# Three opening groups of idle TensorE products: six of 512 columns each become twelve of 256 columns

## The chip, the cores and the metric

The kernel runs on one core of a Trainium2 chip. The metric is the device time of one execution in microseconds (us); before the change it is 158.09 us, the median of three runs that lie between 158.01 and 158.14 us. One more execution was taken under the hardware profiler. The core has four engines that compute and one that only moves data: TensorE (PE; its weight loads are listed apart as PEld), VectorE (DVE), ScalarE (ACT), GpSimd (POOL) and SyncE (SP). An entry such as PEldq or DVEq is the sequencer of that engine, the part that reads the engine's instruction list and hands the instructions out.

## The reference

Two layers follow each other. The first is a sorted block attention: for each of 4 batches and 8 heads an 8 by 8 matrix is normalized five times over rows and columns, mixes the eight blocks of 96 tokens of K and V, and each block of Q attends to its mixed block. The second is a gated layer whose gate is a product over the sequence.

```python
for _ in range(5):
    P = np.exp(P - np.max(P, axis=-1, keepdims=True))
    P = P / (np.sum(P, axis=-1, keepdims=True) + 1e-09)
    P = P / (np.sum(P, axis=-2, keepdims=True) + 1e-09)
k_sorted = np.einsum('bhij,bhjcd->bhicd', P, k_b)      # v_sorted alike
scores = scale * np.matmul(q_b, k_sb.transpose(0, 1, 2, 4, 3))
attn = softmax(scores);  x = np.matmul(attn, v_sb)     # x: 4 x 768 x 512
h = np.maximum(x @ w_in, 0.0);  u, v = h[..., :512], h[..., 512:]
v_n = (v - mean(v)) / np.sqrt(var(v) + 1e-06)
v_s = np.einsum('ts,bsd->btd', w_spatial, v_n) + b_spatial[None, :, None]
out = (u * v_s) @ w_out                                # 4 x 768 x 512
```

## The kernel before, in words

The program is one long unrolled list of units. ORDER (from line 17) names them in the order in which they are issued, `run` (L785) takes them one by one, and each engine receives its own instructions in that order; nothing is reordered later. Loads and stores go through the queues of POOL, SP and, at the end, ACT. A unit's arguments begin with the PSUM tile (ps0 to ps3) or the engine that empties it.

**The opening.** `CO` fills the tile `warm` with zeros. `SK` is the normalization, a chain between ACT and DVE. `L` issues the loads of q, k, v and of the weights from POOL's queue. `DM:ps:n:w` (`u_DM`, L223) issues n idle products of w columns, each with its own load of the same 128 columns of `warm` as weights; they write to a PSUM tile whose content nobody reads. Three such groups, on ps0, ps2 and ps1, stand first in TensorE's list. Behind them come `QT` (L314, transposes of Q), two more groups on ps0 and ps3, `QT` twice, `PR` (L256, the mixing matrices), a sixth group, and `KT` and `VT` (L383, mixed K and V). From there on TensorE has work without idle products: scores (`SC`, L442), their products with V (`AT`, L488), `XT` (L518), `VP` (L554), `UP` (L597), `SP` (L609) and `OP` (L636), interleaved over the four batches.

**The end.** The last batch is split finely. `SH` (L666) is the product over the sequence, eight groups of six products, in this order of PSUM tiles: 1, 2, 0, 2, 3, 1, 2, 3. The first four groups have 512 columns, the last four 256. DVE empties each into `z` (L672), and `GH` multiplies z by u into `gt` (L679) on POOL or DVE. A group that takes a PSUM tile for the second time waits until DVE has emptied it: the fourth group waits for the z of the second, the seventh for the z of the fourth, the eighth for the z of the fifth. `OH` (L686) is the output product, `OI` copies it out of PSUM and `OJ` (L698) stores it.

**The jump.** Between `SH`/`GH` and `OH` stands `IF`. A flag that was computed on the device says whether the inputs allow the short way of normalizing; each engine loads it (`LF`, L731) and then jumps at L794. If the flag is clear, the engines go to the block "usual", which holds the tail from `OH` on. If not, they run `general_path`, a second, safer version of the whole kernel. In the instruction list of each engine the general path stands directly behind the jump, and "usual" behind the general path, so that the usual case jumps over all of it. For TensorE, VectorE and ScalarE the unit `BH` (L734) gives the jump a hint that it will likely be taken.

A product of TensorE is two instructions, a weight load and the product. TensorE's compiled list has 1633 such pairs before the jump; a few semaphore and register instructions lie between them, seven of them between 20 us and the jump.

The lines that matter:

```python
223:    def u_DM(ps, n, w):
225:        for _ in range(int(n)):
226:            nc.tensor.matmul(t[:, 0, 0:int(w)], lhsT=warm[:, 0:128], rhs=warm[:, 0:int(w)], start=True, stop=True)
791:        head, tail = ORDER.split("IF")
794:        with tc.If(st["beyond"] < 1, preferred_fallthrough_block=False, label="usual") as usual:
```

Of the kernel before, what the change touches and what calls it, by code (L numbers as in the profile page):

```python
# [16 lines left out]

ORDER = """
IV:0 CO S0 SK:0 SK:1 LH:S:0 L:q:0:4:8 L:k:0:0:8 L:v:0:0:8 SK:2 IV:2 ID MA L:v:1:0:8 MC QC:A:1 SK:3 L:k:1:0:8 MB QC:A:0
DM:0:6:512 L:q:1:0:8 DM:2:6:512 DM:1:6:512 QT:3:A:0:1 SK:4 QT:2:A:0:3 DM:0:6:512 DM:3:6:512 L:wv QT:1:A:0:0 QT:2:A:0:2  # L20
PR:0 P0:0:2 L:wu P0:6:8 P0:2:4 DM:3:6:512 P0:4:6 PC:D KT:1:D:0:1 PD:1:4:8 KT:3:A:0:0 L:wsb L:wsa KT:0:D:0:3 KT:2:A:0:2
IV:1 L:v:2:0:8 VT:1:A:0:0 VT:3:D:0:1 PD:1:0:4 SC:0:0:0:0 SC:2:0:0:1 VB:1:D:0:0 L:k:2:0:8 VB:3:D:0:1 SC:0:0:1:0
VT:1:A:0:2 AT:2:0:0:0 VT:3:A:0:3 PD:2:4:8 AT:0:0:1:0 L:q:2:0:8 VM:1:A:1:0 VB:2:D:0:2 SC:3:0:1:1 XT:0:D:0:0:0
AT:1:0:0:1 SC:2:0:2:0 VM:3:A:1:3 VB:0:D:0:3 PD:2:0:4 SC:1:0:2:1 AT:2:0:2:0 KT:3:D:1:1 KT:0:D:1:2 SC:1:0:3:0 VM:2:A:1:1
SC:3:0:3:1 AT:1:0:1:1 KT:2:A:1:3 KT:0:A:1:0 AT:3:0:3:0 VM:1:A:1:2 PD:3:4:8 QQ:2:D:1:0 XT:3:D:0:1:0 L:k:3:0:8
AT:0:0:3:1 XT:1:A:0:0:2 QQ:2:A:1:2 AT:3:0:2:1 VP:1:A:0:0:1 XT:0:D:0:1:2 ST:0:1 VP:2:D:0:2 ST:0:0 SC:0:1:1:1 SC:3:1:2:1
L:q:3:0:8 VC:1:4:8 VP:1:D:0:4:5 SC:2:1:3:1 ST:0:4 ST:0:5 SC:3:1:3:0 VP:0:A:0:3 SC:2:1:0:1 ST:0:2 UP:1:A:0:1:1
AT:0:1:1:1 L:v:3:0:8 SC:3:1:0:0 ST:0:3 UP:2:A:0:0:0 AT:0:1:3:1 AT:1:1:2:1 LN:0:0:6 UP:3:A:0:0:1 AT:0:1:0:1 LA:0:5
WW:2:A:0 WW:1:D:4 XT:3:A:1:1:2 UP:0:A:0:1:0 LA:0:2 VC:1:0:4 AT:2:1:0:0 VM:1:A:2:1 BI WW:3:D:2 SC:0:1:2:0 VM:2:A:2:2
XT:1:D:1:1:0 LA:0:0 BH LA:0:4 LA:0:1 LA:0:3 VM:3:A:2:0 SC:0:1:1:0 VP:1:A:1:4:5 AT:2:1:3:0 AT:0:1:1:0 ST:1:5 SP:3:0:2  # L30
AT:0:1:2:0 L:wo SP:1:0:0 VM:2:D:2:3 SP:0:0:1 VC:2:4:8 XT:3:D:1:0:2 XT:1:A:1:0:0 VC:2:0:4 QQ:2:D:2:0 KT:0:A:2:1
KT:3:D:2:0 GT:D:0:0 QQ:1:D:2:2 KT:2:A:2:2 KT:0:A:2:3 PD:3:0:4 GT:P:0:2 VP:3:A:1:0:1 SC:1:2:0:1 SC:2:2:0:0 SP:0:0:3
ST:1:4 SC:3:2:2:1 SC:1:2:1:1 ST:1:1 VP:2:A:1:2:3 KT:3:D:3:2 QQ:0:D:3:0 ST:1:2 SC:1:2:3:0 UP:2:A:1:1:0 AT:0:2:0:1
GT:P:0:3 KT:3:A:3:0 ST:1:3 QQ:1:D:3:2 SC:0:2:3:1 AT:2:2:2:1 UP:3:D:1:0:1 VM:1:A:3:3 UP:0:A:1:0:0 AT:2:2:3:1
UP:3:A:1:1:1 GT:P:0:1 ST:1:0 LN:1:0:6 AT:2:2:1:1 AT:0:2:3:0 XD:2:1 LA:1:4 OP:1:0:0 AT:2:2:0:0 OE:A:0:0 OP:0:0:2
SC:2:2:2:0 LA:1:2 LA:1:5 OE:D:0:2 SC:1:2:1:0 LA:1:1 LA:1:0 LA:1:3 OP:3:0:4 AT:1:2:1:0 AT:0:2:2:0 SP:2:1:2 VM:0:D:3:1
VM:1:D:3:0 OE:A:0:4 VP:3:D:2:4:5 KT:0:A:3:1 KT:2:D:3:3 SP:1:1:3 VM:0:A:3:2 GT:D:1:3 OS:0:0 ST:2:4 SP:3:1:1 SC:2:3:3:1
SC:1:3:1:1 XD:2:0 OS:0:2 GT:D:1:2 ST:2:5 SP:0:1:0 VC:3:4:8 SC:3:3:2:1 SC:2:3:0:1 UP:1:D:2:1:0 GT:D:1:1 VC:3:0:4
VP:3:A:2:2:3 AT:1:3:3:1 GT:P:1:0 VP:2:A:2:0:1 ST:2:3 AT:1:3:2:1 AT:3:3:1:1 UP:0:A:2:1:1 OP:1:1:0 ST:2:0 ST:2:1 ST:2:2
OE:A:1:0 AT:2:3:0:1 LN:2:0:6 LA:2:1 UP:0:D:2:0:0 SC:1:3:0:0 LA:2:3 SC:3:3:1:0 LA:2:2 LA:2:5 LA:2:0 OP:2:1:4 AT:1:3:0:0  # L40
AT:3:3:1:0 XD:3:1 OE:A:1:4 OP:0:1:2 LA:2:4 SC:1:3:3:0 OE:D:1:2 SC:3:3:2:0 SP:2:2:2 AT:1:3:2:0 UP:0:A:2:0:1 AT:3:3:3:0
CK VP:2:A:3:4:5 GT:D:2:2 OS:1:2 SP:1:2:1 ST:3:5 OS:1:4 XD:3:0 SP:3:2:3 SP:2:2:0 ST:3:4 CF:3 GT:D:2:1 GT:P:2:3
UP:0:A:3:1:0 VP:2:D:3:2:3 VP:3:A:3:0:1 ST:3:0 ST:3:1 ST:3:2 UP:2:A:3:0:1 GT:P:2:0 LF OP:1:2:2 ST:3:3 OE:A:2:2 LN:3:0:6
OP:0:2:0 LA:3:4 LA:3:5 OS:2:2 OE:A:2:0 UP:3:D:3:1:1 LA:3:2 LA:3:0 OP:2:2:4 LA:3:3 OE:A:2:4 LA:3:1 OS:2:4 UP:0:A:3:0:0
SH:1:3:3:0 GH:P:3:3:0 SH:2:3:0:0 GH:D:3:0:0 SH:0:3:1:0 SH:2:3:2:0 SH:3:3:1:1 GH:P:3:1:0 SH:1:3:0:1 GH:P:3:2:0 OS:1:0
GH:P:3:1:1 SH:2:3:3:1 SH:3:3:2:1 OS:2:0 GH:P:3:0:1 GH:D:3:2:1 GH:D:3:3:1 OS:0:4 IF OH:1:3:2:0:512:0:4
OH:2:3:3:0:512:0:4 OH:0:3:4:0:256:0:4 OI:A:3:2:0:512 OI:A:3:3:0:512 OH:3:3:5:0:256:0:4 OI:D:3:4:0:256 OI:D:3:5:0:256
OJ:3:2:0:512:S OJ:3:3:0:512:S OJ:3:4:0:256:S OJ:3:5:0:256:A OH:2:3:5:256:512:0:4 OH:1:3:1:0:512:0:4
OH:3:3:4:256:512:0:4 OI:D:3:5:256:512 OI:A:3:1:0:512 OJ:3:5:256:512:S OI:A:3:4:256:512 OJ:3:4:256:512:S OJ:3:1:0:512:A
OH:2:3:0:0:512:0:4 OI:A:3:0:0:512 OJ:3:0:0:512:S  # L50
"""


# [774 lines left out]
```

## Time and profile before

| what | value |
|---|---|
| median of three runs | 158.09 us |
| the profiled execution's own time | 158.44 us |
| its span, first to last instruction | 156.6 us |
| TensorE products (PE), busy | 147.9 us, 94% |
| VectorE, busy | 120.3 us, 77% |
| ScalarE, busy | 81.8 us, 52% |
| GpSimd, busy | 36.8 us, 23% |
| idle products (L226) | 11.0 us |

Times in the profile count from the first instruction. A row of the timeline gives start, duration, engine, line, operation, the tiles written and read, how many instructions were merged, and in brackets how long the engine stood idle before and what the profile holds to have ended that. A wait for several things at once is put down to the one that came last; "issue" means that nothing which the profile shows was waited for. The durations of products are modelled and overlap, so that short stops of TensorE show less in them than in the starts. Instructions of the sequencer (jumps, semaphores, register loads) are not counted as busy and not in the counts of the engines. A row by windows gives, for a stretch of time, the busy us of each engine and in parentheses its number of instructions, then the granted clock of TensorE, the mean busy share of the 16 DMA engines and the rate in GB/s. A few records of products are missing; weight loads are complete.

### The profile page before, as it was taken

What the parts mean: (1) busy time and instruction counts of PE and PEld (TensorE: products, weight loads), DVE (VectorE), ACT (ScalarE), POOL (GpSimd) and SP (SyncE); (2) the same over time, 40 slices, a digit from 0 to 9 for tenths busy, and PEclk for the clock granted to TensorE, in tenths of its full rate; (3) what the DMA queues carried; (4) which work ended last, traced back from release to release, by engine and by line L of the source; (5) the groups of instructions that cost most, each with busy time, mean ns of one, the idle gap of its engine ahead of it and who ended that gap; (6) DMA issues with size and microseconds to landing.
All of it is one profiled execution on the core that took longest, in us unless ns stands there. A gap on an engine that the chain in (4) does not pass through costs nothing.

```text
span 156.6 us, 3974 instructions
## 1 busy us (share of the span) xinstructions
PE 147.9 (94%) x1650; PEld 89.8 (57%) x1665; DVE 120.3 (77%) x270; ACT 81.8 (52%) x112; POOL 36.8 (23%) x43
## 2 busy tenths in 40 slices
PE   6999898999999999999999999999999999999590
PEld 2356776854676669567655565555565544546360
DVE  4777789869998799389898889899969796837530
ACT  3465988867889405867456044547432026440051
POOL 7922955534000040061000000400000440016400
PEclk9999999999999999999999999999999999999999
DMA  3999999999999999990035536500478000359065
GB/s 76 264 204 204 204 204 205 208 217 239 276 210 203 204 204 204 248 193 0 0 63 175 105 136 110 97 0 17 88 268 98 7 0 0 134 196 343 14 217 184
DMA packets 27653, 23.57 MB, mean 150 GB/s; under 512 B 7280, under 2 KB 24688, under 8 KB 27632
## 3 DMA queue, kind: packets, MB, share of 16 engines
q0 software_dynamic: 14352, 11.80, 47.5%
q1 hardware_dynamic: 12992, 11.10, 25.8%
q10 hardware_dynamic: 288, 0.39, 0.7%
q8 instruction: 14, 0.23, 0.6%
q14 instruction: 7, 0.06, 0.1%
HBM read 24.78 MB, written 6.29 MB: 198 GB/s over the span
## 4 chain that ended last, share of the span: by engine, by line
PE 83%; DMA 8%; ACT 2%; issue 2%; DVE 1%; POOL 1%; DVEq 0%; ACTq 0%; POOLq 0%
PE ps L609 15%; PE ps L597 14%; PE ps L554 13%; PE ps L636 10%; DMA v_in<-in_v_dram 8%; PE ps L488 5%; PE ps L666 5%; PE ps L442 4%; PE ps L383 4%; PE ps L686 3%; PE ps L314 3%; PE ps L410 2%; PE ps L518 2%; PE ps L531 1%; PE ps L401 1%
## 5 line engine op out<-in xcount | busy, mean ns | idle before, releaser
L447 ACT ACTIVATE ex<-ps 96x768 bf16<-96x768 f32 x32 | 24.8, 805 | 8.7 <-PE ps L442 8.6
L626 POOL TENSOR_TENSOR gt<-z,u_sb 128x768 bf16<-128x768 f32 x6 | 9.8, 1642 | 78.8 <-DVE z L615 61.2
L609 PE MATMUL ps<-wspT,v_sb 128*128 128x384 bf16 x144 | 25.1, 327 | 0.0
L597 PE MATMUL ps<-xT,w_in_sb 128*128 128x384 bf16 x128 | 23.5, 327 | 0.0
L496 DVE TENSOR_TENSOR x_sb<-ps,rec_all 96x512 bf16<-96x512 f32 x32 | 22.0, 687 | 1.1
L554 PE MATMUL ps<-w_in_sb,xT 128*128 128x512 bf16 x87 | 22.1, 380 | 0.6 <-issue 0.2
L609 PEld LDWEIGHTS <-v_sb 128*128 128x128 bf16 x144 | 13.5, 98 | 8.9
L115 ACT COPY o_sb<-ps 128x1024 f32<-128x1024 f32 (+2 forms) x12 | 9.7, 816 | 17.0 <-PE ps L686 11.9
L571 DVE BATCH_NORM_STATS2 stats<-v_sb 128x6 f32<-128x512 bf16 x24 | 16.3, 678 | 2.0 <-ACT v_sb L121 1.5
L636 PE MATMUL ps<-w_out_sb,gt 128*128 128x512 bf16 x68 | 16.7, 379 | 0.2
L615 DVE TENSOR_TENSOR z<-ps,b_bc 128x768 f32<-128x768 f32 x12 | 11.4, 952 | 7.0 <-PE ps L609 6.8
L121 ACT ACTIVATE u_sb<-ps 128x768 bf16<-128x768 f32 x12 | 9.7, 810 | 13.1 <-PE ps L597 13.0
L597 PEld LDWEIGHTS <-w_in_sb 128*128 128x128 bf16 x128 | 11.6, 97 | 7.4
L554 PEld LDWEIGHTS <-xT 128*128 128x128 bf16 x96 | 8.7, 98 | 9.3 <-issue 0.2
L121 ACT ACTIVATE v_sb<-ps 128x1024 bf16<-128x1024 f32 (+1 forms) x9 | 8.8, 975 | 8.7 <-PE ps L554 8.7
L488 PEld LDWEIGHTS <-ex 96*128 96x128 bf16 x256 | 10.6, 97 | 3.9 <-issue 0.4
L488 PE MATMUL ps<-vb,ex 96*128 96x65 bf16 x256 | 12.2, 193 | 0.3 <-issue 0.3
L226 PE MATMUL ps<-warm 128*128 128x512 bf16 x35 | 11.0, 477 | 1.3 <-DVE warm L199 1.3
L636 PEld LDWEIGHTS <-gt 128*128 128x128 bf16 x72 | 6.6, 97 | 7.2
L115 ACT CAST kt<-ps 128x768 bf16<-128x768 f32 x9 | 6.9, 800 | 6.5 <-PE ps L383 6.5
L442 PE MATMUL ps<-qT,kt 64*128 64x96 bf16 x256 | 9.3, 204 | 0.5 <-DVE kt L117 0.4
L442 PEld LDWEIGHTS <-kt 64*128 64x128 bf16 x256 | 6.2, 94 | 5.8 <-issue 3.9
(94 smaller groups left out, 208.3 us busy)
## 6 DMA issues: line engine op xcount, KB each, us to landing
out_dram<-o_sb SPq DMA_DIRECT2D x9, 512.0 KB, 3.7
k_in<-in_k_dram POOLq DMA_DIRECT2D x4, 768.0 KB, 23.0
v_in<-in_v_dram POOLq DMA_DIRECT2D x4, 768.0 KB, 22.1
vb<-vm SPq DMA_DIRECT2D x24, 99.0 KB, 6.6
q_in<-in_q_dram POOLq DMA_DIRECT2D x3, 768.0 KB, 29.6
ws_in<-in_moe_w_spatial_dram POOLq DMA_DIRECT2D x2, 576.0 KB, 22.3
w_in_sb<-in_moe_w_in_dram POOLq DMA_DIRECT2D x2, 512.0 KB, 24.1
q<-in_q_dram SPq DMA_DIRECT2D x1, 768.0 KB, 4.6
```

Of the source, the lines that this page charges most:

```text
L115: nc.scalar.copy(out=out, in_=in_)
L121: nc.scalar.activation(out=out, in_=in_, func=AF.Relu)
L442: nc.tensor.matmul(t[:, hh, 0:HW].rearrange("p (g x) -> p g x", g=G)[:, :, ii * TB:(ii + 1) * TB], lhsT=kT[rows, i * BLK:i * BLK + 128], r ...
L447: nc.scalar.activation(out=e_tile(b, hp, ih).rearrange("p h (x g) -> p h x g", g=G), in_=t[0:BLK, :, 0:HW].rearrange("p h (g x) -> p h x g ...
L488: nc.tensor.matmul(t[:, hh, ii * VW:ii * VW + D + 1], lhsT=e[:, c:c + 128], rhs=vb[b % 2][:, ih * NI + ii, 2 * hp + hh, 0:D + 1], start=Tr ...
L496: nc.vector.tensor_mul(out=x_sb[:, hp].rearrange("p i (h d) -> p h i d", h=2), in0=tv[:, :, :, 0:D], in1=_raw_ap(rec, 0, [rec.ap[0], [NI, ...
L554: nc.tensor.matmul(t[:, x, :], lhsT=st["xT", b][:, n // 3, kc, (n % 3) * 128:(n % 3 + 1) * 128], rhs=w_in_sb[:, kc, DH:DFF], start=(kc == ...
L571: nc.vector.bn_stats(out=stats, in_=st["v_sb", b, n])
L597: nc.tensor.matmul(t[:, x, 0:HW], lhsT=w_in_sb[:, kc, mc * 128:(mc + 1) * 128], rhs=st["xT", b][:, ih, kc, :], start=(kc == 0), stop=(kc = ...
L609: nc.tensor.matmul(t[:, x, 0:HW], lhsT=st["v_sb", b, n][:, mc * 128:(mc + 1) * 128], rhs=wspT[:, 3 * x:3 * x + 3, n, :], start=(n == 0), s ...
L615: nc.vector.tensor_add(out=z.rearrange("p (x c) -> p x c", x=2), in0=t[:, :, 0:HW], in1=b_bc.rearrange("p (x c) -> p x c", x=2),)
L636: nc.tensor.matmul(t[:, x, :], lhsT=st["gt", b, mc][:, (n0 + x) * 128:(n0 + x + 1) * 128], rhs=w_out_sb[:, mc, :], start=(mc == 0), stop=( ...
```

## The change

The first three groups of idle products are cut finer: twelve products of 256 columns each instead of six of 512. The columns are the same in sum, 3 x 3072. TensorE's list gets 18 weight loads and 18 products more, 36 instructions, all of them ahead of everything else that TensorE does, and so also ahead of its jump. The three later groups keep their six products of 512 columns. No unit is added, taken away or moved, and the other engines' lists stay as they are. In the text of ORDER the lines are broken differently behind this place, with the same units in the same order.

```diff
-DM:0:6:512 L:q:1:0:8 DM:2:6:512 DM:1:6:512 QT:3:A:0:1 SK:4 QT:2:A:0:3 DM:0:6:512 DM:3:6:512 L:wv QT:1:A:0:0 QT:2:A:0:2
+DM:0:12:256 L:q:1:0:8 DM:2:12:256 DM:1:12:256 QT:3:A:0:1 SK:4 QT:2:A:0:3 DM:0:6:512 DM:3:6:512 L:wv QT:1:A:0:0
...
```

More of the change, by code (lines that the diff above doesn't have):

```diff
@@ L19 @@
 IV:0 CO S0 SK:0 SK:1 LH:S:0 L:q:0:4:8 L:k:0:0:8 L:v:0:0:8 SK:2 IV:2 ID MA L:v:1:0:8 MC QC:A:1 SK:3 L:k:1:0:8 MB QC:A:0
-DM:0:6:512 L:q:1:0:8 DM:2:6:512 DM:1:6:512 QT:3:A:0:1 SK:4 QT:2:A:0:3 DM:0:6:512 DM:3:6:512 L:wv QT:1:A:0:0 QT:2:A:0:2
-PR:0 P0:0:2 L:wu P0:6:8 P0:2:4 DM:3:6:512 P0:4:6 PC:D KT:1:D:0:1 PD:1:4:8 KT:3:A:0:0 L:wsb L:wsa KT:0:D:0:3 KT:2:A:0:2
-IV:1 L:v:2:0:8 VT:1:A:0:0 VT:3:D:0:1 PD:1:0:4 SC:0:0:0:0 SC:2:0:0:1 VB:1:D:0:0 L:k:2:0:8 VB:3:D:0:1 SC:0:0:1:0
-VT:1:A:0:2 AT:2:0:0:0 VT:3:A:0:3 PD:2:4:8 AT:0:0:1:0 L:q:2:0:8 VM:1:A:1:0 VB:2:D:0:2 SC:3:0:1:1 XT:0:D:0:0:0
@@ L24 @@
[L24 to L48, printed above, removed]
@@ L49 @@
-OH:3:3:4:256:512:0:4 OI:D:3:5:256:512 OI:A:3:1:0:512 OJ:3:5:256:512:S OI:A:3:4:256:512 OJ:3:4:256:512:S OJ:3:1:0:512:A
-OH:2:3:0:0:512:0:4 OI:A:3:0:0:512 OJ:3:0:0:512:S
+DM:0:12:256 L:q:1:0:8 DM:2:12:256 DM:1:12:256 QT:3:A:0:1 SK:4 QT:2:A:0:3 DM:0:6:512 DM:3:6:512 L:wv QT:1:A:0:0
+QT:2:A:0:2 PR:0 P0:0:2 L:wu P0:6:8 P0:2:4 DM:3:6:512 P0:4:6 PC:D KT:1:D:0:1 PD:1:4:8 KT:3:A:0:0 L:wsb L:wsa KT:0:D:0:3
+KT:2:A:0:2 IV:1 L:v:2:0:8 VT:1:A:0:0 VT:3:D:0:1 PD:1:0:4 SC:0:0:0:0 SC:2:0:0:1 VB:1:D:0:0 L:k:2:0:8 VB:3:D:0:1
@@ new lines @@
+SC:0:0:1:0 VT:1:A:0:2 AT:2:0:0:0 VT:3:A:0:3 PD:2:4:8 AT:0:0:1:0 L:q:2:0:8 VM:1:A:1:0 VB:2:D:0:2 SC:3:0:1:1
+XT:0:D:0:0:0 AT:1:0:0:1 SC:2:0:2:0 VM:3:A:1:3 VB:0:D:0:3 PD:2:0:4 SC:1:0:2:1 AT:2:0:2:0 KT:3:D:1:1 KT:0:D:1:2
+SC:1:0:3:0 VM:2:A:1:1 SC:3:0:3:1 AT:1:0:1:1 KT:2:A:1:3 KT:0:A:1:0 AT:3:0:3:0 VM:1:A:1:2 PD:3:4:8 QQ:2:D:1:0
+XT:3:D:0:1:0 L:k:3:0:8 AT:0:0:3:1 XT:1:A:0:0:2 QQ:2:A:1:2 AT:3:0:2:1 VP:1:A:0:0:1 XT:0:D:0:1:2 ST:0:1 VP:2:D:0:2
+ST:0:0 SC:0:1:1:1 SC:3:1:2:1 L:q:3:0:8 VC:1:4:8 VP:1:D:0:4:5 SC:2:1:3:1 ST:0:4 ST:0:5 SC:3:1:3:0 VP:0:A:0:3 SC:2:1:0:1
@@ new lines @@
+ST:0:2 UP:1:A:0:1:1 AT:0:1:1:1 L:v:3:0:8 SC:3:1:0:0 ST:0:3 UP:2:A:0:0:0 AT:0:1:3:1 AT:1:1:2:1 LN:0:0:6 UP:3:A:0:0:1
+AT:0:1:0:1 LA:0:5 WW:2:A:0 WW:1:D:4 XT:3:A:1:1:2 UP:0:A:0:1:0 LA:0:2 VC:1:0:4 AT:2:1:0:0 VM:1:A:2:1 BI WW:3:D:2
+SC:0:1:2:0 VM:2:A:2:2 XT:1:D:1:1:0 LA:0:0 BH LA:0:4 LA:0:1 LA:0:3 VM:3:A:2:0 SC:0:1:1:0 VP:1:A:1:4:5 AT:2:1:3:0
+AT:0:1:1:0 ST:1:5 SP:3:0:2 AT:0:1:2:0 L:wo SP:1:0:0 VM:2:D:2:3 SP:0:0:1 VC:2:4:8 XT:3:D:1:0:2 XT:1:A:1:0:0 VC:2:0:4
+QQ:2:D:2:0 KT:0:A:2:1 KT:3:D:2:0 GT:D:0:0 QQ:1:D:2:2 KT:2:A:2:2 KT:0:A:2:3 PD:3:0:4 GT:P:0:2 VP:3:A:1:0:1 SC:1:2:0:1
@@ new lines @@
+SC:2:2:0:0 SP:0:0:3 ST:1:4 SC:3:2:2:1 SC:1:2:1:1 ST:1:1 VP:2:A:1:2:3 KT:3:D:3:2 QQ:0:D:3:0 ST:1:2 SC:1:2:3:0
+UP:2:A:1:1:0 AT:0:2:0:1 GT:P:0:3 KT:3:A:3:0 ST:1:3 QQ:1:D:3:2 SC:0:2:3:1 AT:2:2:2:1 UP:3:D:1:0:1 VM:1:A:3:3
+UP:0:A:1:0:0 AT:2:2:3:1 UP:3:A:1:1:1 GT:P:0:1 ST:1:0 LN:1:0:6 AT:2:2:1:1 AT:0:2:3:0 XD:2:1 LA:1:4 OP:1:0:0 AT:2:2:0:0
+OE:A:0:0 OP:0:0:2 SC:2:2:2:0 LA:1:2 LA:1:5 OE:D:0:2 SC:1:2:1:0 LA:1:1 LA:1:0 LA:1:3 OP:3:0:4 AT:1:2:1:0 AT:0:2:2:0
+SP:2:1:2 VM:0:D:3:1 VM:1:D:3:0 OE:A:0:4 VP:3:D:2:4:5 KT:0:A:3:1 KT:2:D:3:3 SP:1:1:3 VM:0:A:3:2 GT:D:1:3 OS:0:0 ST:2:4
@@ new lines @@
+SP:3:1:1 SC:2:3:3:1 SC:1:3:1:1 XD:2:0 OS:0:2 GT:D:1:2 ST:2:5 SP:0:1:0 VC:3:4:8 SC:3:3:2:1 SC:2:3:0:1 UP:1:D:2:1:0
+GT:D:1:1 VC:3:0:4 VP:3:A:2:2:3 AT:1:3:3:1 GT:P:1:0 VP:2:A:2:0:1 ST:2:3 AT:1:3:2:1 AT:3:3:1:1 UP:0:A:2:1:1 OP:1:1:0
+ST:2:0 ST:2:1 ST:2:2 OE:A:1:0 AT:2:3:0:1 LN:2:0:6 LA:2:1 UP:0:D:2:0:0 SC:1:3:0:0 LA:2:3 SC:3:3:1:0 LA:2:2 LA:2:5
+LA:2:0 OP:2:1:4 AT:1:3:0:0 AT:3:3:1:0 XD:3:1 OE:A:1:4 OP:0:1:2 LA:2:4 SC:1:3:3:0 OE:D:1:2 SC:3:3:2:0 SP:2:2:2
+AT:1:3:2:0 UP:0:A:2:0:1 AT:3:3:3:0 CK VP:2:A:3:4:5 GT:D:2:2 OS:1:2 SP:1:2:1 ST:3:5 OS:1:4 XD:3:0 SP:3:2:3 SP:2:2:0
@@ new lines @@
+ST:3:4 CF:3 GT:D:2:1 GT:P:2:3 UP:0:A:3:1:0 VP:2:D:3:2:3 VP:3:A:3:0:1 ST:3:0 ST:3:1 ST:3:2 UP:2:A:3:0:1 GT:P:2:0 LF
+OP:1:2:2 ST:3:3 OE:A:2:2 LN:3:0:6 OP:0:2:0 LA:3:4 LA:3:5 OS:2:2 OE:A:2:0 UP:3:D:3:1:1 LA:3:2 LA:3:0 OP:2:2:4 LA:3:3
+OE:A:2:4 LA:3:1 OS:2:4 UP:0:A:3:0:0 SH:1:3:3:0 GH:P:3:3:0 SH:2:3:0:0 GH:D:3:0:0 SH:0:3:1:0 SH:2:3:2:0 SH:3:3:1:1
+GH:P:3:1:0 SH:1:3:0:1 GH:P:3:2:0 OS:1:0 GH:P:3:1:1 SH:2:3:3:1 SH:3:3:2:1 OS:2:0 GH:P:3:0:1 GH:D:3:2:1 GH:D:3:3:1
+OS:0:4 IF OH:1:3:2:0:512:0:4 OH:2:3:3:0:512:0:4 OH:0:3:4:0:256:0:4 OI:A:3:2:0:512 OI:A:3:3:0:512 OH:3:3:5:0:256:0:4
@@ L51 @@
+OI:D:3:4:0:256 OI:D:3:5:0:256 OJ:3:2:0:512:S OJ:3:3:0:512:S OJ:3:4:0:256:S OJ:3:5:0:256:A OH:2:3:5:256:512:0:4
+OH:1:3:1:0:512:0:4 OH:3:3:4:256:512:0:4 OI:D:3:5:256:512 OI:A:3:1:0:512 OJ:3:5:256:512:S OI:A:3:4:256:512
+OJ:3:4:256:512:S OJ:3:1:0:512:A OH:2:3:0:0:512:0:4 OI:A:3:0:0:512 OJ:3:0:0:512:S
 """
```

## The prediction

> **What bounds the kernel now.** I read the page first, then the chain of work that ended last, then the jump, then the two places where TensorE stops without a reason that the profile names.
>
> ```profile
> span 156.6 us, 3974 instructions
> ...
> PE 147.9 (94%) x1650; PEld 89.8 (57%) x1665; DVE 120.3 (77%) x270; ACT 81.8 (52%) x112; POOL 36.8 (23%) x43
> ...
> q8 instruction: 14, 0.23, 0.6%
> ```
>
> TensorE is busy nearly throughout. The last row is a DMA queue that carries instructions, not data: 14 packets with 0.23 MB, 16 KB each. The other number to remember is that an instruction is 64 bytes in the compiled list, so that a packet is a block of 256 instructions.
>
> ```profile
> 3.08 12.82 DMA v_in<-in_v_dram
> 15.94 0.54 PE ps L383 x12
> ...
> 138.26 7.81 PE ps L666 x48
> 146.08 0.03 issue
> ...
> 147.40 0.26 issue
> 147.66 4.71 PE ps L686 x29
> ```
>
> The chain runs through the first V load until 15.94 us, and from there on almost only through TensorE. A gain on TensorE before 15.9 us is worth nothing; a gain behind that reaches the end unless another engine takes it. The largest hole in TensorE's work stands between L666, whose last product ends at 146.06, and L686 at 147.66. The chain puts it down to DVE's gt. The rows about the hole say otherwise:
>
> ```profile
> 138.10 7.96 PE L666 MATMUL ps<-wspT,v_sb 128*128 128x512 bf16 x48
> ...
> 140.89 0.69 DVE L672 TENSOR_TENSOR z<-ps,b_bc 128x512 f32<-128x512 f32 x1 [0.54 <-PE ps L666]
> ...
> 143.12 3.61 POOL L679 TENSOR_TENSOR gt<-z,u_sb 128x512 bf16<-128x512 f32 x4 [1.46 <-DVE z L672]
> 143.55 1.02 DVE L672 TENSOR_TENSOR z<-ps,b_bc 128x512 f32<-128x512 f32 x2 [0.57 <-PE ps L666]
> 144.86 0.42 DVE L672 TENSOR_TENSOR z<-ps,b_bc 128x256 f32<-128x256 f32 x1 [0.29 <-PE ps L666]
> 145.51 0.42 DVE L672 TENSOR_TENSOR z<-ps,b_bc 128x256 f32<-128x256 f32 x1 [0.23 <-POOL gt L679]
> ...
> 146.63 0.76 DVE L679 TENSOR_TENSOR gt<-z,u_sb 128x256 bf16<-128x256 f32 x2
> 147.57 0.83 PEld L686 LDWEIGHTS <-gt 128*128 128x128 bf16 x5 [1.79 <-issue]
> 147.66 1.02 PE L686 MATMUL ps<-w_out_sb,gt 128*128 128x512 bf16 x4 [1.59 <-DVE gt L679]
> ```
>
> The first two output groups (OH on ps1 and ps2) read tokens 256 to 511, so they need only the four gt halves of 512 columns and empty ps1 and ps2. The last of these halves is the second of POOL's four pieces; POOL's last two are half as long, which puts its end at about 143.12 + 2 x 1.20 = 145.5. ps1 is empty at 145.28, ps2 at 145.93. DVE's two late pieces (until 147.39) are for the third group. So TensorE could have gone on at 146.06. What held it is its jump:
>
> ```profile
> L794 ACTq COMPARE_BRANCH  x1: 68/68/68, 138.3 to 138.3; - x1
> ...
> L794 PEldq COMPARE_BRANCH  x1: 2882/2882/2882, 144.6 to 144.6; - x1
> ...
> L794 DVEq COMPARE_BRANCH  x1: 84/84/84, 146.6 to 146.6; - x1
> ```
>
> The same jump takes ACT 68 ns and DVE 84 ns, TensorE 2882 ns: from about 144.64 to 147.52, where the weight load at 147.57 follows. In just that time one block comes in:
>
> ```profile
> 139.00:144.50 5.50, 5.50 (x33) 3.01 (x32) 3.62 (x6) 0.11 (x1) 2.49 (x3) 1.00 1.02 375
> 145.00:147.00 2.00, 1.06 (x10) 0.70 (x8) 1.50 (x5) 0.00 (x0) 1.73 (x3) 1.00 0.04 12
> ```
>
> 12 GB/s over 2 us are 24 KB: about one block of TensorE's (16 KB) and a smaller one of another engine. Before, until 144.5, the stores of the third batch keep the DMA engines busy (share 1.02).
>
> **Where the blocks begin.** TensorE stops once more inside a group of eight L488 products that have no wait between them, after the 223rd weight load:
>
> ```profile
> 19.24 0.27 PEld L488 LDWEIGHTS <-ex 96*128 96x128 bf16 x7
> 19.86 0.10 PEld L488 LDWEIGHTS <-ex 96*128 96x128 bf16 x1 [0.36 <-issue]
> 19.25 0.36 PE L488 MATMUL ps<-vb,ex 96*128 96x65 bf16 x6
> 19.86 0.22 PE L488 MATMUL ps<-vb,ex 96*128 96x65 bf16 x2 [0.26 <-issue]
> 0.00:14.10 14.10, 12.77 (x93) 5.70 (x96) 8.86 (x52) 7.46 (x13) 7.80 (x16) 1.00 1.03 185
> 0.00:19.60 19.60, 17.79 (x221) 9.98 (x223) 13.31 (x57) 11.94 (x20) 12.59 (x22) 1.00 1.11 191
> 0.00:146.80 146.80, 142.58 (x1619) 86.71 (x1633) 118.51 (x266) 79.14 (x107) 36.79 (x43) 1.00 0.77 150
> ```
>
> I read this as the edge of a block that came late. From there to the jump are 1633 - 223 = 1410 loads, 1411 products (one load was ahead of its product) and seven sequencer instructions of the compiled list, 2828 = 11 x 256 + 12. So the jump stands 12 instructions into a block, which are exactly the six pairs of the eighth L666 group. The sequencer comes to this block only when the seventh group is let through, by the z of the fourth, at about 144.24 (the first of the two at 143.55); the jump's target is there at 147.52, 3.28 us later.
>
> My theory: entering the block that holds the hinted jump makes the sequencer order the target's block, once. ACT and DVE entered theirs long before, TensorE 0.4 us before the jump, and it pays the rest.
>
> **The change part by part.** *The idle products.* 18 x 512 and 36 x 256 columns are the same columns.
>
> ```profile
> 1.28 6.87 PE L226 MATMUL ps<-warm 128*128 128x512 bf16 x18 [1.28 <-DVE warm L199]
> 1.68 0.15 PEld L226 LDWEIGHTS <-warm 128*128 128x128 bf16 x1 [0.28 <-issue]
> 2.11 0.15 PEld L226 LDWEIGHTS <-warm 128*128 128x128 bf16 x1 [0.28 <-issue]
> 8.07 0.86 PE L314 MATMUL ps<-ident,q_in 128*64 128x128 bf16 x24
> 15.94 0.47 PE L383 MATMUL ps<-pd,v_in 128*64 128x128 bf16 x10 [0.37 <-DMA v_in<-in_v_dram]
> 21.95 0.37 PEld L518 LDWEIGHTS <-x_sb 96*128 96x128 bf16 x8
> 21.96 0.51 PE L518 MATMUL ps<-ident,x_sb 96*128 96x96 bf16 x8
> ```
>
> One product takes 0.43 us there (2.11 - 1.68), half of it 0.21, and a weight load 0.15 fits under that. If the 18 added loads lay bare, they would cost 18 x 0.15 = 2.7 us, less the 0.37 us that TensorE waits for V at 15.94: 2.3 us. The nearest row against it is L518, where eight products of 96 columns with a load each pass in 0.51 us, their loads under them. I take 0; the cover is the product itself, and behind it the 0.37 us.
>
> *The early stop.* All block edges move 36 instructions forward in the work. The block after the one that stops now was ordered when its forerunner was entered, 128 pairs before the edge, at the 95th load, just before 14.10; it was usable at 19.86, 5.8 us later, with DMA busy all the time. After the change that forerunner begins 36 instructions sooner, behind the idle products at about 12.1, so the next block is usable at 17.9, and its edge is reached at about 18.5. The stop goes: 0.45 us between the product starts 19.41 and 19.86. It is worth between 0 and 0.45, for ACT is nearly full there and takes part of it; I take 0.2.
>
> *The jump.* It stands 48 instructions into its block, and these are the last four L666 groups. The block is entered when the fourth group is let through, by the z of the second: 140.89 + 0.69 = 141.58 instead of 144.24, 2.66 us sooner. The target then comes between 141.58 + 3.28 = 144.86 (as now) and 141.58 + 5.8 = 147.4 (as under the loads of the opening), since the stores run until 144.5. The middle is 146.1, and I take that: the block in question is one packet, and the stores are a single burst. TensorE goes on at 146.1 instead of 147.66, 1.5 us sooner. The ends are 1.6 us gained (no sooner than 146.06) and 0.2 (147.4 instead of 147.57). Late next is DVE's gt at 147.39 for the third output group, which then begins at about 146.1 + 1.7 = 147.8: 0.4 us of room. Everything behind is TensorE, copies and stores, and moves as a whole.
>
> Sum: -1.5 - 0.2 + 0 = -1.7 us. The profiled execution took 158.44 us, which gives 156.7; the median of the runs lies 0.35 us lower, which gives 156.4.
>
> **The rivals.** *A, the stores hold the block back.* It is ordered in the middle of the burst (375 GB/s), and the opening showed 5.8 us under load. With 5 us it is there at 146.6 and the gain is 1.0 + 0.2: 156.9; with 5.8 it is 0.2 + 0.2: 157.7. For it: share 1.02. Against: 1.32 would be the like of the opening only with many more, smaller packets.
>
> *B, the block is ordered by the jump itself.* Then it does not matter where the jump stands; 2.88 us stay, and only the early stop goes: 157.9, or 158.1 without. The change would do nothing at the place that it moves. For it: the page alone can't tell an order at 144.24 from one at 144.64. Against it: 84 and 68 ns of DVE and ACT for the same jump over a whole second kernel. [...]
>
> *C, slower: two blocks in a row.* If entering a block orders the following block first, and the target only after it, the present 12 instructions leave no time for the former, while 48 do. Then the following block, useless here, is ordered at 141.58 and can hold up the target, ordered at 144.64. This decides if the first comes late, at 147.4, so that the second starts behind it: 147.4 + 2.88 = 150.3 instead of 147.52, 2.8 us more, less 0.2: 160.7. Against: TensorE has only 14 packets in all, none of them for a block behind the jump.
>
> **How the numbers follow.** My case (1.2 us or more of the jump's 1.6 gained) 0.50; A with 0.3 to 1.2 us in all 0.20; B 0.17; C and bare weight loads together 0.13. Runs of this kernel tell 0.2%, 0.3 us, from nothing. Faster: my case, A, and a little of B, 0.72; same: most of B, 0.15; slower: 0.13. The time is 156.4, my case's. Below, 1.6 + 0.45 gives 156.0; with a run's scatter 155.9. Above, the range takes in A and B to 158.2 and leaves out C.
>
> **What the profile after would show.** Right: TensorE's jump takes some 0.1 us to 1.4 us instead of 2.88; the first L686 product follows L666 within 0.1 us, or begins where the block lands; the L488 group at 19.4 us is whole; the first Q transpose (L314) still begins near 8.07; still 14 instruction packets. A shows a jump of 1.5 to 2.8 us with an unchanged start at 144.6; B one of 2.88; C 15 packets. Wrong would be the whole if L314 began a microsecond later, or if L686 waited for something other than the jump.

## The result, and the profile after

The changed kernel takes 157.00 us, the median of 20 executions between 156.23 and 158.40 us, against 158.19 us of the kernel before beside it on the same chip (20 executions, 157.97 to 158.69). The ratio is 0.9926, with a 95% interval of 0.9900 to 0.9952: faster by 1.2 us, where the forecast had 1.7.

The 20 executions don't scatter evenly. Eight lie at 156.23 to 156.42 us, seven at 156.99 to 157.29, five at 158.11 to 158.40; those of the kernel before all lie within 0.7 us. In the upper five the mean granted clock of TensorE is 0.984 to 0.989, in the others at least 0.995. The profiled execution is one of the upper kind: 158.39 us, clock 0.989. It is as long as the profiled one of before (158.44 us), and that is what makes it worth reading: the tail has won all that the prediction hoped for, and something ahead has lost as much.

The page of the changed kernel: span, engines, granted clock over 40 slices, and the queue that carries code.

```profile
span 156.6 us, 4025 instructions
...
PE 148.7 (95%) x1683; PEld 92.8 (59%) x1683; DVE 120.4 (77%) x270; ACT 81.8 (52%) x112; POOL 36.9 (24%) x43
...
PEclk9999879999999999999999999999999999999999
...
q8 instruction: 14, 0.23, 0.5%
```

Still 14 packets of code. In the clock row the 8 and the 7, fifth and sixth of 40, cover 15.7 to 23.5 us.

**The tail.** The jump of the changed kernel on the three sequencers that showed it before:

```profile
L794 ACTq COMPARE_BRANCH  x1: 68/68/68, 140.0 to 140.0; - x1
...
L794 PEldq COMPARE_BRANCH  x1: 481/481/481, 146.3 to 146.3; - x1
...
L794 DVEq COMPARE_BRANCH  x1: 84/84/84, 148.4 to 148.4; - x1
```

The timeline of the same kernel around it:

```profile
139.81 7.96 PE L666 MATMUL ps<-wspT,v_sb 128*128 128x512 bf16 x48
...
142.60 0.69 DVE L672 TENSOR_TENSOR z<-ps,b_bc 128x512 f32<-128x512 f32 x1 [0.53 <-PE ps L666]
...
147.61 2.65 PE L686 MATMUL ps<-w_out_sb,gt 128*128 128x512 bf16 x15
...
148.34 0.76 DVE L679 TENSOR_TENSOR gt<-z,u_sb 128x256 bf16<-128x256 f32 x2
```

TensorE's jump takes 481 ns instead of 2882, and it lies beside products that are still queued: L686 begins at 147.61, where L666 ends (147.77 in the modelled ends), while DVE's two late gt pieces only start at 148.34. So the bracket of before that put the hole down to DVE's gt was wrong, as the prediction read it. From the first L666 product to the first of L686 the kernel before took 147.66 - 138.10 = 9.56 us, this one 7.80: 1.76 us less.

**The opening.** The finer idle products cost nothing by themselves: the first Q transposes (L314) begin no later than before, at 7.45 us against 8.07.

```profile
1.28 5.78 PE L226 MATMUL ps<-warm 128*128 128x256 bf16 x36 [1.28 <-DVE warm L199]
7.45 0.86 PE L314 MATMUL ps<-ident,q_in 128*64 128x128 bf16 x24 [0.39 <-ACT q_in L115]
```

That they begin sooner is not the change's doing. In this execution the idle products go to double speed at 4.74 us, where its clock record starts at full rate (one every 0.21 us until then, every 0.11 from there); in the profiled execution of before that is at 6.99 us. Over all fourteen profiles on record this moment lies between 3.99 and 6.99 us, and the nine with the old opening have the Q transposes at 7.35 to 8.07. At full rate the products of 256 columns follow each other every 0.11 us, half of the 0.22 of those with 512, and their weight loads take 0.098 us (median), so no weight load lies bare there either.

All that the tail won is missing again at 139.81, where L666 begins 1.71 us later than before (138.10). The chain and then TensorE's timeline of the changed kernel show from where:

```profile
3.08 13.68 DMA v_in<-in_v_dram
...
16.80 0.55 PE ps L383 x12
```

```profile
16.80 0.86 PE L383 MATMUL ps<-pd,v_in 128*64 128x128 bf16 x24 [1.85 <-DMA v_in<-in_v_dram]
17.59 0.52 PE L442 MATMUL ps<-qT,kt 64*128 64x96 bf16 x16
18.22 1.81 PE L401 MATMUL ps<-ident,vT 128*96 128x128 bf16 x16
...
21.18 0.62 PE L488 MATMUL ps<-vb,ex 96*128 96x65 bf16 x8
...
23.67 0.52 PE L518 MATMUL ps<-ident,x_sb 96*128 96x96 bf16 x8
```

V lands at 16.75 us instead of 15.90, and TensorE is idle 1.85 us ahead of it. The 16 products of L401 then take 1.81 us; in the kernel before the same row reads

```profile
17.36 1.14 PE L401 MATMUL ps<-ident,vT 128*96 128x128 bf16 x16
```

The eight L488 products are whole now, as forecast, and yet at L518 the kernel is 1.71 us behind (23.67 against 21.96). Nothing is lost after that, until the jump. The windows of the changed kernel, cut where the clock turns (columns: length, busy time and count of PE, PEld, DVE, ACT, POOL, then granted clock, DMA share, GB/s):

```profile
14.98:18.39 3.41, 1.48 (x43) 1.24 (x44) 1.52 (x2) 1.86 (x4) 2.90 (x6) 1.00 1.31 201
18.39:21.80 3.41, 3.41 (x46) 2.86 (x46) 1.64 (x3) 2.44 (x4) 1.88 (x2) 0.50 1.32 204
21.80:25.20 3.40, 3.40 (x69) 2.66 (x70) 3.23 (x8) 3.07 (x5) 1.54 (x2) 1.00 1.32 205
```

For 3.41 us TensorE runs at half clock, right behind a stretch of the same length in which it was busy for only 1.48 us. In the kernel before that stretch has 2.93 us of products, and the clock stays at 1.00:

```profile
14.98:18.39 3.41, 2.93 (x78) 2.49 (x72) 2.75 (x4) 3.35 (x5) 3.39 (x6) 1.00 1.32 206
```

Why V is late stands in the DMA view. The first answer is for the kernel before, the second for the changed one, both for 14.2 to 15.9 us, the last microseconds of V's transfer:

```profile
q0 software_dynamic: 457, 0.34, 131.2%
```

```profile
q0 software_dynamic: 440, 0.33, 126.8%
q8 instruction: 1, 0.02, 3.5%
q14 instruction: 1, 0.01, 1.2%
```

A block of TensorE's code, 16 KB in one packet, now comes in while V is still loading. Before, that block came at 17.54 us, behind V. The packets' starts, and when the last of V's 16 parts had landed, from the list of packets in the traces (us; "opening" is new where the first three groups of idle products are those of the changed kernel):

```
kernel (profiled run)   opening  block starts  V landed
before                  old      17.54         15.90
late16, late24, late40  old      17.0 - 17.6   15.83 - 15.92
changed                 new      14.72         16.75
changed, once more      new      14.40         16.47
after_fill4             new      14.64         16.67
after_fill4_more        new      14.95         15.90
front36_late216         new      14.71         16.75
```

The packet takes 0.95 us on one of the 16 DMA engines, and one part of V comes up to 0.85 us later: in the changed kernel 15 of the 16 parts have landed by 15.87 us and the last at 16.75; before, 15 by 15.36 and the last at 15.90. In one of the five V is on time. There the packet starts last of the five, at 14.95, just as V's first part lands (14.96); in the others it starts ahead of that. It is the 36 instructions that bring the block forward, and not the time of the full clock: in all nine profiles with the old opening it starts at 16.77 to 17.59 us.

### The profile page after: what moved, and what is told of

Same layout as the page of the kernel before. It is cut to its first block, busy times and chain, and to the rows that moved or that the text cites. A ratio compares the mean times of both kernels' runs of the same rounds, so it can differ in the third digit from the quotient of the medians.

```text
span 156.6 us, 4025 instructions
## 1 busy us (share of the span) xinstructions
PE 148.7 (95%) x1683; PEld 92.8 (59%) x1683; DVE 120.4 (77%) x270; ACT 81.8 (52%) x112; POOL 36.9 (24%) x43
## 4 chain that ended last, share of the span: by engine, by line
PE 84%; DMA 9%; ACT 2%; POOL 1%; DVE 1%; issue 1%; ACTq 0%; POOLq 0%
PE ps L609 15%; PE ps L597 14%; PE ps L554 14%; PE ps L636 10%; DMA v_in<-in_v_dram 9%; PE ps L488 5%; PE ps L666 5%; PE ps L442 4%; PE ps L383 4%; PE ps L686 3%; PE ps L314 3%; PE ps L410 2%; PE ps L518 2%; PE ps L401 1%; PE ps L531 1%; POOL q_in L169 1%
## 5 line engine op out<-in xcount | busy, mean ns | idle before, releaser
L597 PE MATMUL ps<-xT,w_in_sb 128*128 128x384 bf16 x128 | 23.5, 326 | 0.0
L554 PE MATMUL ps<-w_in_sb,xT 128*128 128x512 bf16 x96 | 22.7, 380 | 0.0
L597 PEld LDWEIGHTS <-w_in_sb 128*128 128x128 bf16 x128 | 11.6, 98 | 7.4
L554 PEld LDWEIGHTS <-xT 128*128 128x128 bf16 x96 | 8.7, 98 | 9.3
L488 PEld LDWEIGHTS <-ex 96*128 96x128 bf16 x256 | 10.7, 98 | 3.6 <-issue 0.2
L488 PE MATMUL ps<-vb,ex 96*128 96x65 bf16 x256 | 12.3, 195 | 0.0
L226 PE MATMUL ps<-warm 128*128 128x256 bf16 (+1 forms) x54 | 10.0, 353 | 1.3 <-DVE warm L199 1.3
```

What stands on the lines that cost most here:

```text
L488: nc.tensor.matmul(t[:, hh, ii * VW:ii * VW + D + 1], lhsT=e[:, c:c + 128], rhs=vb[b % 2][:, ih * NI + ii, 2 * hp + hh, 0:D + 1], start=Tr ...
L554: nc.tensor.matmul(t[:, x, :], lhsT=st["xT", b][:, n // 3, kc, (n % 3) * 128:(n % 3 + 1) * 128], rhs=w_in_sb[:, kc, DH:DFF], start=(kc == ...
L597: nc.tensor.matmul(t[:, x, 0:HW], lhsT=w_in_sb[:, kc, mc * 128:(mc + 1) * 128], rhs=st["xT", b][:, ih, kc, :], start=(kc == 0), stop=(kc = ...
```

## The experiments

Three questions stood open. Is it the position of the jump in its block that decides? What holds the block back in the kernel before: the time of its order, the stores, or the jump itself (B)? And what does the new opening cost?

Most kernels are the kernel before with its old opening and a few instructions more in the third batch of L554 and L597: so many groups of four products of 512 columns (384 in L597) are cut into halves, which adds eight instructions per group and no columns. This moves the jump in its block and leaves everything ahead of 20 us alone.

```diff
+    left = {"groups": N}
+    def parts(b, w):
+        if b < 2 or left["groups"] == 0:
+            return [slice(0, w)]
+        left["groups"] -= 1
+        return [slice(0, w // 2), slice(w // 2, w)]
...
-            for kc in range(KC):
-                nc.tensor.matmul(t[:, x, :], ...)
+            for c in parts(b, DFF - DH):
+                for kc in range(KC):
+                    nc.tensor.matmul(t[:, x, c], ...)
```

**Eight, 16 and 24 instructions more** (N = 1, 2, 3; the jump stands 20, 28 and 36 instructions into its block, 12 before).

> Before, with the opening untouched; one group of four 512-column products of the third batch (L554) is done as eight of 256 columns, so that the jump stands 20 instructions into its block instead of 12. Theory (the block is entered when the last waiting group ahead of it is let through, and only then the target is ordered): the block now begins inside the seventh group of L666, behind its first product, which waits for the z of the fourth group; so it is entered at the same moment as before, the jump takes 2.8 to 3.0 us and the time is that of before, within 0.2 us. Rival, every instruction of distance counts in proportion: 8 instructions more are about 0.5 us, the jump takes 2.4 us and the kernel is 0.5 us faster. Rival B (the jump itself orders the block): 2.88 us, no change.

> As before, but two groups of four 512-column products of the third batch are cut in two: 16 instructions more ahead of the jump, none of them in the opening; the jump stands 28 instructions into its block. Theory: the block now begins inside the sixth group, ahead of the seventh group's wait, and is entered when the fourth group is let through, 2.6 us sooner: jump 0.5 us or less, no hole ahead of L686, 1.5 us faster than before (156.6 against 158.1), all runs alike, since the opening is untouched. Proportional rival: jump 1.9 us, 1.0 us faster. Rival B: 2.88 us, no change.

> Three groups of four products of the third batch cut in two: 24 instructions more, the jump 36 into its block. 28 still cost 2.88 us and 52 cost 0.48. Theory, mended: the target is ordered some instructions after the entry of the block, not at its first one; six at least. At 36 the block begins with the sixth L666 group; if the order is given within the first 12 instructions it falls ahead of the seventh group's wait: jump 0.48 us, 156.6. If later, it falls behind that wait: jump about 2.9 us, 158.2. Rival (the order follows in steps of distance): a jump between 0.5 and 2.8 us.

late8 takes 158.19 us (ratio 0.9994, 0.9985 to 1.0002), late16 158.27 (1.0002, 0.9992 to 1.0013), late24 158.22 (0.9997, 0.9987 to 1.0006). None is faster. In late24 the jump is as long as ever, and the hole stands behind it; the jump and TensorE's timeline of late24:

```profile
L806 PEldq COMPARE_BRANCH  x1: 2861/2861/2861, 144.5 to 144.5; - x1
```

```profile
147.51 1.24 PE L697 MATMUL ps<-w_out_sb,gt 128*128 128x512 bf16 x5 [1.57 <-DVE gt L690]
```

late8's jump takes 2881 ns, as expected; late16, with 2881 ns too, misses the 0.5 us or less that was expected of it. At position 28 the block begins in the sixth L666 group, which the z of the second lets through, and by the prediction that should have won most of the 1.6 us. Either the order goes out later than the prediction has it, or the block then takes longer to come than its middle value: from that z to the end of the jump late16 has 147.34 - 141.40 = 5.9 us, close to rival A's 5.8. The runs without stores, below, bear on this.

**Thirty-two and 40 more** (N = 4, 5; positions 44 and 52).

> Four groups cut in two: 32 instructions more, the jump 44 into its block. With the mended theory: 0.48 us and 156.6, if the order is given within the first 20 instructions of the block; else 2.9 us and 158.2.

> As before, but five groups of four products of the third batch are cut in two: 40 instructions more ahead of the jump, none in the opening; the jump stands 52 into its block. Theory: no better than 28, since the block is again entered when the fourth group is let through or at most a group sooner: jump 0.5 us or less, 1.5 us faster than before, and all runs within 0.4 us of each other, whereas the changed kernel's runs lie at 156.3, 157.0 and 158.4. If instead those three values come from the tail (the stores that run while the block is fetched), this kernel spreads as widely as the changed one. Rival B: no change.

late32 takes 156.69 us (0.9899, 0.988 to 0.9919; two executions), late40 156.48 (0.9881, 0.9867 to 0.9895). The jump of late32, then of late40:

```profile
L806 PEldq COMPARE_BRANCH  x1: 392/392/392, 144.4 to 144.4; - x1
```

```profile
L806 PEldq COMPARE_BRANCH  x1: 481/481/481, 144.7 to 144.7; - x1
```

Eight instructions between late24 and late32 decide over 1.5 us: the position is what counts, and it acts as a step. late40 has no new opening, so it shows the price of the jump alone, 1.8 us (158.24 - 156.48), and it is the fastest of all kernels that ran; its interval ends just below that of the changed kernel's 20 executions (0.9895 against 0.9900). Its early stop is still there:

```profile
19.81 0.22 PE L495 MATMUL ps<-vb,ex 96*128 96x65 bf16 x2 [0.19 <-issue]
```

late32's two executions, 156.42 and 156.97 us, both at full clock, lie 0.55 us apart with the old opening; the lower two values of the changed kernel lie 0.7 us apart. What parts them no run here shows, so not all of the spread need come from the opening.

**A whole block more** (32 groups, from the first batch on: 256 instructions, so the position is 12 again), with the old opening and, with 27 groups behind the new opening (252 in all, position 8), with the new one.

> As before, but 32 groups of four products (L554 of all batches, L597 of the last two or so) are cut in two: 256 instructions more ahead of the jump, one whole block, so that the jump stands 12 into its block again. Theory: the jump takes 2.8 to 3.0 us as in the kernel before, though far more instructions were added than in the change; the time is that of before, plus 0 to 0.4 us for 128 more starts. A rival by which any added instructions ahead of the jump help (more of them, more time for the fetch): a short jump and 1.5 us faster.

> The opening of the changed kernel (36 instructions more there), and 27 groups of four products further on cut in two, 216 instructions more, so that the jump stands 8 instructions into its block, as badly as before. Theory: the jump takes 2.88 us again. The opening alone decides the rest: in the profile of the changed kernel the second code block after the start is ordered sooner and its 16 KB run at 14.7 us through one of the DMA engines that still carry V of the first batch; V lands at 16.75 instead of 15.90, TensorE stands idle 1.85 us and in some runs the clock halves behind that. So this kernel should show the three values of the changed kernel (156.3, 157.0, 158.4) about 1.6 us higher: 157.9, 158.6, 160.0, plus 0 to 0.4 for 108 more starts as in the kernel with 256 more. Rival (the three values come from the tail): one value, about 158.8, as that kernel had.

late256 takes 158.80 us (1.0028, 1.0016 to 1.0040), its jump 2861 ns. Its page has one packet of code more, 15 instead of 14; a packet is 16,384 bytes in the trace of the kernel before, which fits 256 instructions of 64 bytes. So 32 more win 1.5 us and 256 more win nothing: what counts in these runs is the position modulo 256 (2882 and 2861 ns at 12, 392 to 481 at 44 to 56), and not how much stands ahead of the jump. The 128 added pairs cost some 0.56 us (158.80 against 158.24 in the same set), about 4 ns each. front36_late216 takes 159.13 us (1.0048, 1.0034 to 1.0061); its jump takes 2821 ns as its position says. The profiled execution is its longest, 160.35 us at a clock of 0.988 (the other six lie at 158.76 to 159.31), and its opening shows what the changed kernel's does, in TensorE's timeline:

```profile
16.79 0.86 PE L390 MATMUL ps<-pd,v_in 128*64 128x128 bf16 x24 [1.77 <-DMA v_in<-in_v_dram]
...
18.21 1.94 PE L408 MATMUL ps<-ident,vT 128*96 128x128 bf16 x16
```

The new opening is so no gain by itself: with the jump where it was, it is no faster than late256 (the intervals overlap), the early stop's gain included. The expected lowest value, 157.9 plus at most 0.4, is missing: six of the seven lie between 158.76 and 159.31, so the two lower values don't show as such, nor do they all lie at the rival's single 158.8.

**The stores away.** The four stores that run under L666 (two of the third batch, one each of the first and the second) are left out, in the kernel before (position 12) and in late24 (position 36); those parts of the output are not written.

```diff
-... LA:3:3 OE:A:2:4 LA:3:1 OS:2:4 UP:0:A:3:0:0 ... GH:P:3:2:0 OS:1:0
+... LA:3:3 OE:A:2:4 LA:3:1 UP:0:A:3:0:0 ... GH:P:3:2:0
-GH:P:3:1:1 SH:2:3:3:1 SH:3:3:2:1 OS:2:0 GH:P:3:0:1 GH:D:3:2:1 GH:D:3:3:1 OS:0:4 IF
+GH:P:3:1:1 SH:2:3:3:1 SH:3:3:2:1 GH:P:3:0:1 GH:D:3:2:1 GH:D:3:3:1 IF
```

> The kernel before without the four stores of 512 KB each (OS:2:4, OS:1:0, OS:2:0, OS:0:4) that run from 139 to 145 us; these parts of the output are left out. The jump stands 12 into its block. Two accounts of the slow jump are left. (i) At 36 instructions or fewer no order goes out ahead of the jump, and the jump itself orders the block: 2.8 us without the stores too. (ii) The order goes out when the block is entered, and the burst of stores holds the packet back until it ends at 145.0 us, which is where it has begun in all slow kernels: without the stores it starts 0.8 us after the order, at about 142.3 to 145.0, and the jump takes 0.4 to 2.5 us.

> The kernel with three groups cut in two (24 instructions more, the jump 36 into its block, 2.86 us) without the same four stores; these parts of the output are left out. (i), the distance decides and the jump orders the block: 2.86 us. (ii), the stores hold the packet back: the block is entered when the fourth group is let through, at about 141.4, the packet starts at about 142.2 and the jump takes 0.4 to 0.5 us.

before_nost takes 156.68 us (0.9902, 0.9882 to 0.9922), late24_nost 156.75 (0.9906, 0.9886 to 0.9926). The jump, the timeline and the windows of the kernel before without these stores:

```profile
L794 PEldq COMPARE_BRANCH  x1: 502/502/502, 144.4 to 144.4; - x1
```

```profile
142.66 3.21 PE L666 MATMUL ps<-wspT,v_sb 128*128 128x512 bf16 x26
145.71 2.54 PE L686 MATMUL ps<-w_out_sb,gt 128*128 128x512 bf16 x14
```

```profile
139.00:142.00 3.00, 3.00 (x15) 1.35 (x14) 1.89 (x3) 0.00 (x0) 1.16 (x1) 1.00 0.01 3
142.50:145.00 2.50, 2.50 (x22) 1.95 (x21) 1.64 (x4) 0.00 (x0) 2.03 (x2) 1.00 0.03 7
```

TensorE's list and the position are the same, and the hole is gone: 502 ns. This is what B could not give; by it the block is ordered by the jump, and stores that end about when the jump begins would not matter. The 7 GB/s of the second window are a block that comes in ahead of the jump at 144.4. The list of packets puts the three cases side by side. S is the first weight load of L666; "packet - S" and the last column, the start of the last store's last data packet (some 0.09 us long), count from there.

```
kernel           position  S       packet starts  jump     packet - S   last store packet - S
before           12        137.94  145.06         2882 ns  7.12         7.05
late16           28        137.76  144.90         2881 ns  7.14         7.05
late24           36        137.81  144.93         2861 ns  7.12         7.08
late32           44        137.67  141.11          392 ns  3.44
late40           52        138.02  142.43          481 ns  4.41
changed          48        139.65  144.05          481 ns  4.40
after_fill4      56        138.29  139.42          392 ns  1.13
before_nost      12        137.75  142.55          502 ns  4.80         (no stores)
late24_nost      36        137.65  142.49          822 ns  4.84         (no stores)
```

At positions 12 to 36 the packet waits for the end of the stores, to 0.1 us; without the stores it starts 2.3 us sooner. That is the block that was held back, the mechanism of rival A, but in the kernel before and not in the changed one. The jump of late24_nost is longer than the 0.4 to 0.5 us expected, 822 ns; its packet took 1.31 us, against 1.01 in before_nost. At 44 to 52 it starts in the middle of the stores, at 56 about as they begin. Why an order that much sooner gets in amid the same burst, while the later one waits for its end, no run here shows. The steps fit an order that goes out while the sequencer is held at a wait and reads ahead some 15 to 22 instructions, an estimate of mine from the positions: the fourth group's first product, which waits for the second group's z, stands 59 instructions ahead of the jump (five groups of twelve, less one), 15 ahead of a block that begins at 44 and 23 ahead of one at 36. The order would then go out, at positions up to 36, when the wait for the second group's z ends (141.39 in before_nost, the packet 1.16 us later), from 44 to 52 one wait sooner, at the third group, and at 56 sooner still. No run shows an order itself or a reading ahead; both are argued from the packets' starts.

**The new opening, filled.** Four idle products of 512 columns stand ahead of the first V transposes, where TensorE waits (position 56). The kernel ran twice, and the changed kernel once more beside it.

```diff
-KT:2:A:0:2 IV:1 L:v:2:0:8 VT:1:A:0:0 ...
+KT:2:A:0:2 IV:1 L:v:2:0:8 DM:1:4:512 VT:1:A:0:0 ...
```

> The changed kernel with four more idle products of 512 columns (0.86 us) between the mixed K and the mixed V of the first batch, where TensorE waits for V. Theory: they cover half of the 1.85 us in which TensorE stands idle, the clock is no longer halved, and the runs at 158.4 vanish; those at 156.3 and 157.0 stay: none over 157.4, granted clock 0.995 or more in all. Rival (the clock falls for another reason than this idle time): one run in five is at 158.4 with a clock of 0.989, as in the changed kernel.

> The same kernel as the changed one with four idle products ahead of the first mixed V, for more values: theory, none over 157.5 and no clock under 0.99, as in the six runs so far; rival, one in five at 158.4.

> The changed kernel once more, for more of its values and one more profile. Theory: about half of the runs near 156.3, a third near 157.0, the rest near 158.4; a profiled run at 156.3 shows the block's packet behind the V load of the first batch (V lands at 15.9), one at 157.0 shows V at 16.7 with the clock at full rate throughout, one at 158.4 V at 16.7 and a halved clock for 3.4 us. The jump is 0.4 to 0.5 us in each.

after_fill4 takes 157.01 us (0.9922, 0.9909 to 0.9935), the second time 157.02 (0.9921, 0.9906 to 0.9935); the changed kernel the second time 156.84 (0.9922, 0.9892 to 0.9952). Of eleven executions with the filling none is over 157.44 us or has a clock under 0.995; of the changed kernel's 26 six lie at 158.05 to 158.40 with a clock of 0.984 to 0.989. That is what a filling should do if idle time halves the clock, though eleven without one would come by chance 6 times in 100. V's lateness it can't mend, and the middle value of 157.0 stays. Where V is on time (after_fill4_more, 156.75 us in the profile) the four products are themselves in the way: the V products begin at 16.43 us, with V there since 15.90, so that a filled kernel can't show 156.3 either. Of the six new executions of the changed kernel only one is near 156.3 (156.29), where about half were expected; 156.67, 156.82 and 156.86 lie between the values of the first 20. TensorE's timeline with the filling, and then that of the changed kernel the second time, which ran at full clock (156.82 us):

```profile
15.05 1.02 PE L226 MATMUL ps<-warm 128*128 128x512 bf16 x4
16.71 0.86 PE L383 MATMUL ps<-pd,v_in 128*64 128x128 bf16 x24 [0.64 <-DMA v_in<-in_v_dram]
```

```profile
16.51 0.86 PE L383 MATMUL ps<-pd,v_in 128*64 128x128 bf16 x24 [1.61 <-DMA v_in<-in_v_dram]
17.30 0.51 PE L442 MATMUL ps<-qT,kt 64*128 64x96 bf16 x16
17.93 0.86 PE L401 MATMUL ps<-ident,vT 128*96 128x128 bf16 x11
```

In the second, V is 0.57 us late (16.51 against 15.94), and L666 begins 138.09 - 137.94 = 0.15 us late; with the filling it is 0.77 and 138.29 - 137.94 = 0.35. Both times 0.42 us are won back between, which is the early stop. The second one idled 1.61 us without its clock being halved; the two profiles with the halved clock idled 1.85 us (changed) and 1.77 (front36_late216).

## Why the prediction was right, and where it was not

**The hole is the jump (right).** 2882 ns became 481, and L686 follows L666 without a hole, ahead of DVE's gt.

**The position of the jump in its block (right).** The step between 36 and 44, the same jump at 12 with 256 instructions more, and a block that comes 2.8 us sooner in the opening all follow from edges 256 instructions apart, which the prediction counted from one stop at 19.4 us; late256's one packet more is a block of that size.

**When the block is ordered (wrong, and it didn't show).** I put the order at the entry of the block and the present delay down to a late order: 144.24 us before, 141.58 after, and 3.28 us from there on. Without its stores the kernel before has the block in time at the same position: the packet starts at 142.55, and the z of the fourth group, my moment of the order, ends at 144.05 in that run. So the order was out at least 1.5 us ahead of what I took, and the stores held the block back. For the changed kernel the packet alone doesn't tell (it starts 0.76 us behind the z of the second, 143.29 to 144.05); but in late32, with four instructions less ahead of the jump in its block, it starts 0.21 us before that z ends (141.11 against 141.32), so here too the order is taken to be out sooner. That the sum came out all the same is luck: the change moves the order too, and so past what held it back. With its packet at S + 4.40, and as the late jump of the kernel before ends 2.46 us behind its packet's start (145.06 to 147.52), the block was usable at about S + 6.86, an estimate from these two runs. With before's S that is 144.8, the lower end of my 144.86 to 147.4. The 1.5 us of the middle were 1.76 in the profiled run, 1.8 in late40's times.

**Rival A** fell as a forecast and held as a mechanism: I asked whether stores hold the block back after the change, and not whether they did so already. (Only two of the four stores are the third batch's, as I had read all of them.) The median of 157.0 lies at its 156.9 only by chance: its jump of 1.5 to 2.8 us isn't there. **Rival B** fell by before_nost: there the target's packet starts 1.9 us ahead of the hinted jump (142.55 against 144.44). **Rival C**, a useless block ahead of the target, fell: 14 packets.

**The early stop (right, somewhat more).** It is gone, and two profiles put it at 0.42 us, the end of my 0 to 0.45, where I took 0.2. In times it is about 0.2: the lowest execution of the changed kernel is 156.23, of late40 156.40.

**The opening at no cost (the step that failed).** I asked when the earlier block would be there for TensorE, and took the 36 instructions at 0 since the products cover them. Bare loads did not come, and that much holds, though my 0.21 us of cover is that of the slow first microseconds; at full clock a product covers its load, 0.098 us, with 0.11. But the block is a transfer, and I didn't ask whose place it takes: it runs amid V, which the chain that I had quoted names as what bounds the kernel until 15.9 us. Of the three values of the changed kernel the lowest, 156.3, is jump and stop together and the forecast's 156.4; the middle one is 0.75 us above, about V's lateness (0.57 to 0.86 us in four of five profiles with the new opening); the upper one has the halved clock besides, 158.4. None of the profiled executions lies at 156.3, so that V is on time there is argued, from after_fill4_more, where it was. Why the packet starts ahead of V's first part in one execution and behind it in the next stays open, and so, in part, does why the clock is halved in some and not in others. The median is therefore 157.0, in the range and 0.6 us over the forecast.

## What to carry to other kernels

Where a sequencer's jump is long in the profile, count its position in its block and look at what the DMA engines carry while the target's block should come: here 32 to 40 instructions more won 1.5 to 1.8 us, four stores left out 1.6, and a jump 44 to 56 instructions into its block took 392 to 481 ns where one at 36 took 2861. But instructions added ahead move later block edges too: the 36 at the front moved a block from 17.54 to 14.72 us, amid V, as a 16 KB packet that took 0.95 us on an engine that carries data too. So look where each lands, and add them late, behind the loads that bound the start: 40 instructions in the third batch won 1.8 us (four executions, 156.4 to 156.8), 36 at the front 1.2 with a spread of 2.2.
